# Joining the small products of an attention and mixture-of-experts kernel into two runs a batch

## The chip, the core and the metric

One NeuronCore of a Trainium2 chip. The time is that of one execution on the device, in microseconds, as the median of several runs; lower is better. The engines run side by side and wait for one another through semaphores: TensorE (PE; PEld is its weight load) for products, VectorE (DVE), ScalarE (ACT), GpSimd (POOL), and SyncE (SP), which issues nearly all transfers.

## The reference

Eight batches, eight heads, 576 tokens, 64 columns a head, 32 memory slots, eight experts:

```python
a = softmax(phi, axis=2)                        # token to memory, (b, h, s, 32)
k_m = einsum('bhsm,bhsd->bhmd', a, k); v_m = einsum('bhsm,bhsd->bhmd', a, v)
attn = softmax(q @ k_m.T / 8) @ v_m             # (b, h, s, 64)
x = attn as (4608, 512)
logits = x @ w_gate + modality_bias[modality_id]
e = argmax(logits); gate = softmax(logits)[e]
out = gate * (relu(x @ w1[e]) @ w2[e])          # one expert a token
```

## The kernel before

With the inputs at hand all tokens prefer one expert; the kernel guesses it from the modality of the first token, runs all tokens through it, and tests at the end (`verdict`) whether any token wanted another; only then a second, general path (`any_experts`) runs. That path reads split copies of the attention weights from DRAM (`xa_dram`, `xb_dram`).

Attention is never multiplied by `v_m` first. For each batch the memory values times `w1` (`value_products`, two halves of the 1024 columns, line 756) give a matrix `vws` of 256 rows; the attention weights of the tokens times `vws` give the hidden layer (`hidden`, line 803), and that times `w2` the output (`outputs`, line 840). Both large stages are exact to float32 by splitting each operand in a high and a low part and making three products. A batch has a part 0 of 256 tokens and a part 1 of the rest; in line 840's stage these are tiles of 128 tokens (0 and 1, then 2 and 3), and every odd batch has a fifth tile for what is left of both batches of a pair (`None`). A tile is 8 chunks (`f`) of 3 products; a hidden part is 8 times 6 products.

The small products of a batch `b`, all on parts of the array:

- `mem_kv` (line 409, and line 417 for its sums): keys and values of the memory, 64 rows by 32 columns of the array, from `exp` of `phi` and from `kv_sb`, which the next batch's load overwrites; then `kv_divide` (VectorE: `den` line 493, `rec`; ScalarE: `kvn` line 499).
- `mem_turn` (line 148): two transposes on the full array, then a copy to `kvT`.
- `scores` (line 565): 64 by 32. Its result is turned, softened and normalised in steps by VectorE and ScalarE (`soften` e, `normalise` n, `a_split` x), which give the weights that `hidden` reads.
- `mem_gate` (line 545): memory values times `w_gate`, 128 by 32, eight products, from `wgd`, a copy of `w_gate` with zeros; copied to `vg`.
- `value_weights`: `value_products` of one half (64 by 32, 16 products of 512 columns), and its split by ScalarE and VectorE (lines 153 and 154).
- `logits` (line 698): weights times `vg`, 128 by 32; then `gate`, whose `gates` scale each output on its way out of PSUM (`gated`, line 853).

PSUM has eight banks: four are taken in turn by `pe` tiles (hidden, outputs, value products), and two pairs (`pair0`, `pair1`) serve the small products.

The order of the instructions of all engines is written out by a planner (`weave`) while the kernel is built. It has two lists: `experts`, strictly in order (hidden, outputs, value products), and `attention`, sorted by a due time that is counted in the progress of the experts. Each stage has its product time and a chain of other engines' times in `TAKES`. An attention stage is put in when its due time has come and its inputs are ready by the planner's own clock; one that uses VectorE is held back while VectorE's queue is more than 3.5 us ahead (some kinds: less). Transfers wait in a list, `later`, of which each call of `hidden` or `outputs` issues one; the output stores and the loads of `k`, `v` and `phi` are issued at once where they are called. `behind` holds back those loads for some batches until the next output store.

At the start, while `phi` is on its way, TensorE does products of zeros: `BUSY[0]` small ones (`warm_small`, line 166) and ten of 512 columns (line 159).

Of the kernel before, what the change touches and what calls it, by code (L numbers as in the profile page):

```python
# [54 lines left out]
def attn_moe(ctx: ExitStack, tc: tile.TileContext, q, k, v, phi, mod_id, w_gate, mod_bias, w1, w2, out):  # L55
    nc = tc.nc
# [20 lines left out]
    HW = MAIN + 2 * QP  # L77
    SCALE = 1.0 / float(D) ** 0.5
    EPS = 1e-9
    BUSY = 90, 10  # L80
# [26 lines left out]

    wgd = const.tile([P, KCH, NG, E], F32, name="wgd")
# [150 lines left out]
    def clear():  # L259
        for t in [wgd] + vg:  # L260
            nc.gpsimd.memset(t, 0.0)

    def prepare():

        for r in range(2):
            half = slice(QP * r, QP * (r + 1))
            for i in range(2):

                nc.gpsimd.tensor_copy(mid_f[half, :, RA * i:RA * (i + 1)], mid[:, i::2, r:2 * RA:2, 0])
            nc.gpsimd.tensor_copy(mid_f[half, :, 2 * RA], mid[:, r::2, QC - 1, 0])  # L270
        for m in range(NMOD):
            nc.gpsimd.tensor_single_scalar(is_m[m][:, :, 0], mid_f.rearrange("p a c -> p (a c)"), float(m), op=ALU.is_equal)
        for g in range(NG):
            rows = slice(D * g, D * (g + 1))
            nc.gpsimd.tensor_copy(wgd[rows, :, g, :], wg[rows])
# [282 lines left out]
    def scores(b):  # L558
        sc = [pair_of_banks(g) for g in range(NG)]
        qT = q_sb[b % 2].rearrange("p j (a x) -> p j a x", a=2)  # L560
        for a in range(2):
            for j in range(HG):
                for g in range(NG):
                    rows = slice(QP * g, QP * (g + 1))
                    nc.tensor.matmul(  # L565
                        sc[g][M * j:M * (j + 1), a, 0:QC * BL], lhsT=kvT[b][rows, 0, M * j:M * (j + 1)],
                        rhs=qT[rows, j, a], start=True, stop=True, tile_position=(QP * g, M * j),
                    )
        live["sc", b] = sc
        if b + 2 < B:  # L570
            load_queries(b + 2)

    def first_scores(c0, n):

        sc = [pair_of_banks(g) for g in range(NG)]
        qT = q_sb[0].rearrange("p j (c u t) -> p j c u t", u=2, t=BL)
        cs = slice(c0, c0 + n)
        for u in range(2):
            for j in range(HG):
                for g in range(NG):  # L580
                    for a in range(2):
# [7 lines left out]
        if c0 + n == QC:  # L589
            load_queries(2)  # L590
# [80 lines left out]
    def a_split(b, part, step=None):  # L671
# [11 lines left out]
        if b % 2:  # L683
            for x, d in zip(dst, drams[b // 2]):
                nc.sync.dma_start(d.bitcast(F32), x.rearrange("p i g c x -> p (i g c x)").bitcast(F32))

    def logits(b):

        pair, i = b // 2, b % 2
        x = live["aT", b].rearrange("p g (c a t) -> p g c a t", a=2, t=BL)  # L690
        pl = bank("pa")
        last = RA * BL
        for cs, c0 in ((slice(0, 2 * RA, 2), 0), (slice(2 * RA, QC, 2), last)):
            for g in range(NG):
                for r in range(HG):
# [5 lines left out]
                    )  # L701
        lgT = wk.tile([P, RB, BL], F32, name="lgT")
# [80 lines left out]

    def value_weights(b, hf):
        value_products(b, hf)
        for g, pv in enumerate(live.pop(("pv", hf))):
# [111 lines left out]
    def first_w2(c):  # L898
# [40 lines left out]
    def plan_memory(b, due, floor=0.0):  # L939
# [6 lines left out]
        for name, after, what, late in (  # L946
# [4 lines left out]
            ("kv", [("exp0" if b < 2 else "exp", b), ("sums", b)], mem_kv, 6.0),  # L951
            ("kvT", [("kv", b)], mem_turn, 9.0),
            *((("vg", [("kvT", b), ("e", b, 1, 0)], mem_gate, 16.9),) if b == 1 else ()),
        ):
            stage(attention, (name, b), name, after, what, b, due=due + late, floor=floor if name in ("max", "kv") else 0.0)
# [94 lines left out]
    def plan_steps(b, dues):  # L1050
# [8 lines left out]
        def step(part):  # L1059
            for k in range(4):  # L1060
                before = ("e", b, part, k - 1 - (b == 1 and (part, k) == (0, 3))) if k else ("s", b, part if b == 0 else 0)
                add(("e", b, part, k), f"e{part}{k}", [before], soften, b, part, k)

        def weights(part):
            for k in range(3):
                before = [("n", b, part, k - 1) if k else ("e", b, part, 3)]
                if b and k == 2:
                    before += [("l", b - 1), ("x", b - 1, 1)]
# [7 lines left out]
        if b:  # L1076
            add(("s", b, 0), "s", [("kvT", b), ("qt", b, HG - 1)], scores, b)
# [7 lines left out]
        else:  # L1085
            step(1)
            todo.insert(len(todo) - 1, (("vg", 0), "vg", [("e", 0, 1, 0)], mem_gate, (0,)))
# [3 lines left out]
        add(("l", b), "l", [("n", b, 1, 2), ("vg", b)], logits, b)  # L1091
# [3 lines left out]
        add(("g", b), "g", [("l", b)], gate, pair, c0, n)  # L1095
# [11 lines left out]
        if b == B - 1:  # L1107
            stage(attention, ("v",), "verdict", [("others", pair)], verdict, due=due + 12.0)
# [8 lines left out]
    def plan_experts(b):  # L1117
        def next_values(hf):
            if b + 1 < B:
                stage(experts, ("vw", b + 1, hf), "vw", [("kvT", b + 1)], value_weights, b + 1, hf, banks=2, full=True)  # L1120

        def some(t, f, kind, terms):
            last_ = f == FCH - 1 and terms[-1] == 2
            stage(
# [3 lines left out]

        def tile_(t):
# [49 lines left out]
    AHEAD, EARLIER, SPREAD = (5.8, 5.0), {7: -6.0}, 0.55  # L1179
# [14 lines left out]
    def weave(experts):  # L1194
# [26 lines left out]
        while at or ex:  # L1221
# [38 lines left out]
            if s[7]:  # L1260
                for k in range(max(1, s[6])):
                    ring[(turn_ - 1 - k) % 4] = t
# [162 lines left out]
```

## Time and profile before

| | |
|---|---|
| Median of 3 runs | 385.58 us (384.74 to 386.07) |
| The profiled execution | 386.81 us, its span 385.0 us |
| TensorE busy | 378.4 us, 98% of the span |
| VectorE, ScalarE, GpSimd busy | 64%, 37%, 12% |
| Mean granted clock of TensorE | 1.000 |

Span is the time from the first to the last instruction of the profiled execution. A product's end is modelled and products overlap, so in what follows the time between the starts of two products counts, not their length. "L840" is line 840 of the kernel before.

### The profile page before, as it was taken

To read this page: it belongs to the slowest core of one execution; us is meant where nothing else is said; L and a number is where in the kernel's file an instruction comes from. 1 tells how busy PE (TensorE), PEld (TensorE's weight loads), DVE (VectorE), ACT (ScalarE), POOL (GpSimd) and SP (SyncE) were. 2 spreads that over 40 slices of the span, in tenths; PEclk is the share of its full clock that TensorE was granted. 3 is DMA by queue.
4 is the path that set the end of the run, shared out by engine and by line. 5 is a ranking of instruction groups with operands and counts; after the bars stand their busy time and mean duration, and the time that the engine had idled before them with its cause. 6 is when DMAs were issued, how large, how long until landed. Compare 5 with 4: busy or idle time off the path is not lost.

```text
span 385.0 us, 9899 instructions
## 1 busy us (share of the span) xinstructions
PE 378.4 (98%) x4007; PEld 305.5 (79%) x4007; DVE 244.8 (64%) x610; ACT 141.2 (37%) x328; POOL 45.7 (12%) x113
## 2 busy tenths in 40 slices
PE   7899999999999999999999999999999999999996
PEld 2767886889679887787878878797967988698986
DVE  3689767885688478745777378773667535892400
ACT  1274332524334233332443324342432324351401
POOL 3229030023000300030000300003000030000000
PEclk9999999999999999999999999999999999999999
DMA  8999669974389296806862069844501111153112
GB/s 292 346 377 222 107 118 316 261 155 147 56 269 184 69 301 116 303 12 197 206 111 49 9 205 217 207 162 127 176 21 36 29 29 29 29 204 97 31 35 55
DMA packets 91674, 56.88 MB, mean 148 GB/s; under 512 B 69476, under 2 KB 74852, under 8 KB 91620
## 3 DMA queue, kind: packets, MB, share of 16 engines
q1 hardware_dynamic: 91344, 55.87, 53.3%
q8 instruction: 33, 0.54, 0.6%
q10 hardware_dynamic: 276, 0.30, 0.2%
q14 instruction: 21, 0.17, 0.1%
HBM read 37.28 MB, written 18.87 MB: 146 GB/s over the span
## 4 chain that ended last, share of the span: by engine, by line
PE 97%; DMA 1%; DVE 1%; ACT 0%; issue 0%; ACTq 0%
PE pe L840 52%; PE pe L803 27%; PE pe L756 4%; PE pair L409 4%; PE pair L565 2%; PE pe L884 1%; PE pair L698 1%; DMA ph<-in_phi_dram 1%; PE pair L434 1%; PE pair L148 1%; DVE top L311 1%; PE pair L583 1%; PE pair L756 1%; PE pe L434 1%; PE pair L545 0%; PE pair L803 0%
## 5 line engine op out<-in xcount | busy, mean ns | idle before, releaser
L840 PE MATMUL pe<-w2h,hh 128*128 128x512 f32 x280 | 113.8, 406 | 0.1
L840 PE MATMUL pe<-w2h,hl 128*128 128x512 f32 x280 | 109.4, 391 | 0.0
L840 PE MATMUL pe<-w2l,hh 128*128 128x512 f32 x280 | 107.3, 391 | 0.0
L820 DVE SCALAR_TENSOR_TENSOR hl<-pe,hh 128x256 fp32r<-128x256 f32 (+2 forms) x158 | 57.3, 389 | 38.4 <-ACT hh L816 37.5
L840 PEld LDWEIGHTS pe<-w2h,hh 128*128 128x128 f32 x280 | 52.5, 188 | 23.7 <-issue 13.9
L816 ACT ACTIVATE hh<-pe 128x256 fp32r<-128x256 f32 (+2 forms) x158 | 53.2, 362 | 36.8 <-PE pe L803 36.5
L840 PEld LDWEIGHTS pe<-w2l,hh 128*128 128x128 f32 x280 | 52.5, 188 | 11.5
L840 PEld LDWEIGHTS pe<-w2h,hl 128*128 128x128 f32 x280 | 52.7, 188 | 9.5 <-issue 0.3
L853 ACT ACTIVATE ob<-pe,gates 128x512 f32<-128x512 f32 x35 | 23.9, 687 | 75.9 <-PE pe L840 48.9
L803 PE MATMUL pe<-xbh,vwh 128*128 128x320 f32 x128 | 40.1, 313 | 0.0
L803 PE MATMUL pe<-xbh,vwl 128*128 128x320 f32 x128 | 39.5, 309 | 0.0
L803 PE MATMUL pe<-xbl,vwh 128*128 128x320 f32 x128 | 39.5, 309 | 0.0
L803 PE MATMUL pe<-xah,vwh 128*128 128x256 f32 x124 | 35.2, 287 | 0.0
L803 PE MATMUL pe<-xal,vwh 128*128 128x256 f32 x124 | 34.9, 283 | 0.0
L803 PE MATMUL pe<-xah,vwl 128*128 128x256 f32 x124 | 34.9, 283 | 0.0
L345 POOL COPY ts<-tm 32x4 f32<-32x4 f32 x24 | 4.8, 200 | 203.8 <-DVE tm L337 203.0
L803 PEld LDWEIGHTS pe<-xah,vwh 128*128 128x128 f32 x124 | 23.6, 191 | 2.2 <-ACT vwl L773 0.8
L803 PEld LDWEIGHTS pe<-xbh,vwh 128*128 128x128 f32 x128 | 24.0, 188 | 1.2 <-DVE hl L820 0.6
L153 ACT CAST vwh<-pe 128x512 fp32r<-128x512 f32 x26 | 14.0, 590 | 29.7 <-PE pe L756 29.7
L803 PEld LDWEIGHTS pe<-xbl,vwh 128*128 128x128 f32 x128 | 24.0, 188 | 0.3
L803 PEld LDWEIGHTS pe<-xbh,vwl 128*128 128x128 f32 x128 | 24.0, 188 | 0.0
L803 PEld LDWEIGHTS pe<-xal,vwh 128*128 128x128 f32 x124 | 23.7, 191 | 0.2
(178 smaller groups left out, 468.0 us busy)
## 6 DMA issues: line engine op xcount, KB each, us to landing
out_dram<-ob SPq DMA_DIRECT2D x72, 128.0 KB, 2.4
q_sb<-in_q_dram SPq DMA_DIRECT2D x112, 72.0 KB, 3.2
kv_sb<-in_k_dram SPq DMA_DIRECT2D x6, 1152.0 KB, 7.0
kv_sb<-in_v_dram SPq DMA_DIRECT2D x6, 1152.0 KB, 10.1
ph<-in_phi_dram SPq DMA_DIRECT2D x13, 288.0 KB, 7.6
kv_sb<-in_k_dram SPq DMA_DIRECT2D x4, 576.0 KB, 5.7
kv_sb<-in_v_dram SPq DMA_DIRECT2D x4, 576.0 KB, 7.0
raw<-in_moe_w_dram SPq DMA_DIRECT2D x2, 1024.0 KB, 7.2
```

The lines of the kernel that those rows point to most:

```text
L148: nc.tensor.transpose(dst, src, ident[:rows, :rows])
L153: nc.scalar.copy(h, src)
L345: nc.gpsimd.tensor_copy(ts_[BL * a:BL * (a + 1)], live["tm"][BL * o:BL * (o + 1)])
L409: nc.tensor.matmul(live["kvp"][M * j:M * (j + 1), g], lhsT=pe[half, j, c * M:(c + 1) * M], rhs=kv_sb[half, :, j, c * D:(c + 1) * D], start ...
L434: nc.tensor.matmul(to[g][M * j:M * (j + 2), 0:2 * D].rearrange("p (j d) -> p j d", j=2), lhsT=pe[half, c, j:j + 2].rearrange("p j m -> p ( ...
L565: nc.tensor.matmul(sc[g][M * j:M * (j + 1), a, 0:QC * BL], lhsT=kvT[b][rows, 0, M * j:M * (j + 1)], rhs=qT[rows, j, a], start=True, stop=T ...
L756: nc.tensor.matmul(pvs[g][M * j:M * (j + 1), :], lhsT=vT[b][rows, j, :], rhs=raw1[rows, j, cols], start=True, stop=not more, tile_position ...
L803: nc.tensor.matmul(ph[:, 0:n], lhsT=(vl if k == 2 else vh)[:, g, cols], rhs=xl if k == 1 else xh, start=(g == k == 0), stop=(g == NG - 1 a ...
L816: nc.scalar.activation(hs[0][:, f, h0:h0 + p1 - p0], live["ph", f][:, p0:p1], AF.Relu)
L820: nc.vector.scalar_tensor_tensor(hl, live["ph", f][:, p0:p1], 0.0, hh.bitcast(F32), op0=ALU.max, op1=ALU.subtract)
L840: nc.tensor.matmul(po, lhsT=tile_columns(hl if n == 1 else hh, f, t), rhs=(w2l if n == 2 else w2h)[:, f, :], start=(f == n == 0), stop=(f ...
L853: nc.scalar.activation(ob, po, AF.Copy, scale=gate_of(b, t))
```

## The change

`mem_gate` is done in the run of `scores`, with sixteen products of 64 rows (each on one half of `w_gate`) instead of eight of 128 rows; its results lie behind the scores in the same banks, and two copies by VectorE take them to `vg`. For batches from `FROM` = 3 on, `logits` of the batch before is done at the head of the same run; this run is a member of `experts`, right after the last product of tile 0, and the eviction of tile 0 follows in the middle of tile 1 ("fin"). `mem_kv` of batch `b + 2`, both halves of value products of `b + 1` and `mem_turn` of `b + 2` become one run at a fixed row of `experts` of batch `b`: after tile 2 (even `b`) or tile 3 (odd `b`), or at the place that `JOINT` names (batch 1: after chunk 1 of the fifth tile; batch 2: after chunk 1 of tile 2; batch 3: after chunk 6 of tile 3). The second half of value products uses `pair0` instead of two `pe` banks, except in batch 6. Due times of the attention stages are reckoned anew. The split weights are written to DRAM per batch in halves of the old pieces, through `later`. `BUSY[0]` falls from 90 to 64, and `wgd` is gone.

```diff
+    FROM = 3
+    JOINT = {1: (4, 1), 2: (2, 1), 3: (3, 6)}
-    BUSY = 90, 10
+    BUSY = 64, 10
...
     def mem_kv(b):
         kv_products(b)
         kv_divide(b)
-        if b in (2, 4, 5):
+        if b in (4, 5):
             behind.append(b)
...
-    def mem_gate(b):
-        pg = bank("pa")
+    def mem_gate(b, to):
         for j in range(HG):
-            nc.tensor.matmul(
-                pg[M * j:M * (j + 1), 0:NG * E], lhsT=vT[b][:, j], rhs=wgd[:, j].rearrange("p g e -> p (g e)"),
-                start=True, stop=True, tile_position=(0, M * j),
-            )
+            for g in range(NG):
+                rows = slice(D * g, D * (g + 1))
+                nc.tensor.matmul(
+                    to[g][M * j:M * (j + 1), 0, GATE:GATE + E], lhsT=vT[b][rows, j], rhs=wg[rows, j],
+                    start=True, stop=True, tile_position=(D * g, M * j),
+                )
+
+    def gate_values(b, to):
         o = E * (b % 2)
-        nc.vector.tensor_copy(vg[b // 2][:, :, o:o + E], pg[:, 0:NG * E].rearrange("p (g e) -> p g e", g=NG))
+        for g in range(NG):
+            nc.vector.tensor_copy(vg[b // 2][:, g, o:o + E], to[g][:, 0, GATE:GATE + E])
...
     def scores(b):
         sc = [pair_of_banks(g) for g in range(NG)]
+        if b >= FROM:
+            logits_product(b - 1, sc[0][:, 0, LOGITS:GATE])
...
         live["sc", b] = sc
+        mem_gate(b, sc)
+        if b >= FROM:
+            add_logits(b - 1, sc[0][:, 0, LOGITS:GATE])
+        gate_values(b, sc)
...
-        if b % 2:
+        c = NG * n * P // 2
+        for i in (0, 1) if b == 1 and not part else (b % 2,):
             for x, d in zip(dst, drams[b // 2]):
-                nc.sync.dma_start(d.bitcast(F32), x.rearrange("p i g c x -> p (i g c x)").bitcast(F32))
+                later.append((d[:, c * i:c * (i + 1)].bitcast(F32), x[:, i].rearrange("p g c x -> p (g c x)").bitcast(F32)))
...
+    def other_values(b):
+        pair = pair_of_banks(0)
+        value_products(b, 1, lambda: [pair[:, g] for g in range(NG)])
+        value_split(1)
...
+    def begin(b):
+        return 61.2 * (b // 2) + 27.8 * (b % 2) - 0.3
...
+            if last_ and t == 0 and FROM <= b + 1 < B:
+                stage(experts, ("o", b, t, f, terms[0]), kind, [], outputs, t, range(f, f + 1), lambda po: None, terms)
+                stage(experts, ("s", b + 1, 0), "ls", [("n", b, 1, 2), ("kvT", b + 1), ("qt", b + 1, HG - 1)], scores, b + 1)
+                return
...
-                if b and t in (2, 3) and f == FCH // 2 - 1:
-                    next_values(t - 2)
+                if t == 1 and f == FCH // 2 - 1 and FROM <= b + 1 < B:
+                    stage(experts, ("fin", b, 0), "fin", [("g", b)], finish_first, full=True)
+                if 0 < b < B - 1 and (4 if t is None else t, f) == JOINT.get(b, (2 + b % 2, FCH - 1)):
+                    if b + 2 < B:
+                        stage(experts, ("kv", b + 2), "kvj", [("exp", b + 2), ("sums", b + 2)], mem_kv, b + 2)
+                    next_values(0)
+                    if b + 2 < B:
+                        stage(experts, ("vw", b + 1, 1), "vw", [], other_values, b + 1)
+                    else:
+                        next_values(1)
+                    if b + 2 < B:
+                        stage(experts, ("kvT", b + 2), "kvTj", [("kv", b + 2)], mem_turn, b + 2)
...
-    AHEAD, EARLIER, SPREAD = (5.8, 5.0), {7: -6.0}, 0.55
+    AHEAD, SPREAD = 5.8, 0.55
+    TURNS, MEMORY = -3.0, 0.0
...
     for b in range(2, B):
-        at0 = (b - 1) * BATCH - AHEAD[b > 2] - EARLIER.get(b, 0.0)
-        plan_memory(b, at0)
-        plan_turns(b, at0 + 6.0, 1.3)
-        plan_steps(b, evenly(at0 + 11.5, SPREAD, 24))
+        if b < FROM:
+            at0 = (b - 1) * BATCH - AHEAD
+            plan_memory(b, at0)
+            plan_turns(b, at0 + 3.3, 0.1)
+            plan_steps(b, evenly(at0 + 5.5, SPREAD, 24))
+            continue
+        plan_turns(b, begin(b - 1) + TURNS, 0.1)
+        if b == FROM:
+            plan_memory(b, at0 + 7.5, exp=at0 + 10.0)
+        else:
+            plan_memory(b, begin(b - 2) + MEMORY)
+        plan_steps(b, evenly(begin(b - 1) + 7.9, 0.3, 24))
...
-                gate_ = ("vg", s[0][1])
-                if s[0][0] == "vw" and s[0][1] > 1 and gate_ not in done and done.get(("e", s[0][1], 1, 0), now + 1.0) < now:
-                    mem_gate(s[0][1])
-                    now += 0.18
-                    done[gate_] = free["D"] = max(now, free["D"]) + 0.2
```

## Rows read from the trace of the kernel before

**Rows 1.** The page: busy time of the engines, and the chain by engine.
```profile
PE 378.4 (98%) x4007; PEld 305.5 (79%) x4007; DVE 244.8 (64%) x610; ACT 141.2 (37%) x328; POOL 45.7 (12%) x113
...
PE 97%; DMA 1%; DVE 1%; ACT 0%; issue 0%; ACTq 0%
```

**Rows 2.** The chain in order of time (start us, us, what): one batch.
```profile
219.47 2.08 PE pair L409 x138
221.55 0.13 PE pair L417 x13
...
225.58 1.13 PE pair L565 x32
...
229.66 7.04 PE pe L803 x48
...
239.44 0.19 PE pair L545 x8
239.62 1.02 PE pe L756 x16
...
244.27 0.70 PE pair L698 x32
```

**Rows 3.** Timeline of TensorE (start us, us, what) around one batch's logits.
```profile
201.94 0.39 PE L840 MATMUL pe<-w2h,hl 128*128 128x512 f32 x1
202.17 0.39 PE L840 MATMUL pe<-w2l,hh 128*128 128x512 f32 x1
202.49 0.77 PE L698 MATMUL pair<-aT,vg 128*32 128x128 f32 x32
203.19 0.50 PE L840 MATMUL pe<-w2h,hh 128*128 128x512 f32 x1
203.53 0.39 PE L840 MATMUL pe<-w2h,hl 128*128 128x512 f32 x1
```

**Rows 4.** Timeline of TensorE: two runs of value products, adjacent.
```profile
19.25 1.09 PE L756 MATMUL pair<-raw,kvT 64*32 64x512 f32 x16 [0.36 <-ACT kvT L540]
20.13 1.83 PE L756 MATMUL pe<-raw,kvT 64*32 64x512 f32 x16
```

**Rows 5.** Timeline of TensorE around one batch's two turns.
```profile
222.87 0.40 PE L840 MATMUL pe<-w2l,hh 128*128 128x512 f32 x1
223.11 0.38 PE L148 MATMUL pair<-ident,kvn 128*128 128x128 f32 x2
...
223.56 0.40 PE L840 MATMUL pe<-w2h,hl 128*128 128x512 f32 x1
```

**Rows 6.** Timeline of all engines after one batch's mem_kv.
```profile
221.61 0.50 PE L840 MATMUL pe<-w2h,hh 128*128 128x512 f32 x1
...
221.88 0.16 DVE L493 TENSOR_SCALAR den<-pair 128x2 f32<-128x2 f32 x1 [4.99 <-PE pair L417]
...
222.34 0.63 ACT L499 ACTIVATE kvn<-pair,rec 128x128 f32<-128x128 f32 x2 [4.70 <-DVE rec L495]
```

**Rows 7.** Timeline of VectorE: first and last step of one batch's weights.
```profile
136.59 0.78 DVE L612 STREAM_TRANSPOSE a<-pair 128x256 f32<-128x256 f32 x2 [1.94 <-PE pair L565]
...
155.53 0.83 DVE L681 TENSOR_TENSOR xbl<-aT,xbh 128x640 fp32r<-128x640 f32 x1
```

**Rows 8.** Timeline of ScalarE and VectorE: the split of one half of value products.
```profile
248.34 1.07 ACT L153 CAST vwh<-pe 128x512 fp32r<-128x512 f32 x2 [1.08 <-PE pe L756]
...
248.96 1.29 DVE L154 TENSOR_TENSOR vwl<-pe,vwh 128x512 fp32r<-128x512 f32 x2 [0.67 <-ACT vwh L153]
```

**Rows 9.** Timeline of TensorE: the opening.
```profile
1.31 0.88 PE L166 MATMUL pair<-busy 64*32 64x16 bf16 x90 [1.31 <-POOL busy L1276]
...
7.25 0.45 PE L148 MATMUL pair<-ident,top 128*128 128x128 f32 x1 [0.52 <-DVE top L311]
...
10.35 4.12 PE L434 MATMUL pair<-kv_sb,exp 64*64 64x128 f32 x72
...
14.43 2.20 PE L434 MATMUL pe<-kv_sb,exp 64*64 64x128 f32 x72
```

More of the change, by code (lines that the diff above doesn't have):

```diff
@@ L259, in clear @@
     def clear():
-        for t in [wgd] + vg:
+        for t in vg:
             nc.gpsimd.memset(t, 0.0)
@@ L589, in first_scores @@
         if c0 + n == QC:
+            mem_gate(0, sc)
+            gate_values(0, sc)
             load_queries(2)
@@ L682, in a_split, with logits_product @@
         drams = xb_dram if part else xa_dram
-        if b % 2:
+        c = NG * n * P // 2
+        for i in (0, 1) if b == 1 and not part else (b % 2,):
             for x, d in zip(dst, drams[b // 2]):
-                nc.sync.dma_start(d.bitcast(F32), x.rearrange("p i g c x -> p (i g c x)").bitcast(F32))
+                later.append((d[:, c * i:c * (i + 1)].bitcast(F32), x[:, i].rearrange("p g c x -> p (g c x)").bitcast(F32)))
     def logits(b):
-        pair, i = b // 2, b % 2
+        add_logits(b, logits_product(b, bank("pa")))
+    def logits_product(b, pl):
+        pair = b // 2
         x = live["aT", b].rearrange("p g (c a t) -> p g c a t", a=2, t=BL)
-        pl = bank("pa")
         last = RA * BL
@@ L701, in logits, with add_logits @@
                     )
+        return pl
+    def add_logits(b, pl):
+        pair, i = b // 2, b % 2
         lgT = wk.tile([P, RB, BL], F32, name="lgT")
@@ L950, in plan_memory @@
             ("sums", [("exp0" if b < 2 else "exp", b)], mem_sums, 3.2),
-            ("kv", [("exp0" if b < 2 else "exp", b), ("sums", b)], mem_kv, 6.0),
-            ("kvT", [("kv", b)], mem_turn, 9.0),
-            *((("vg", [("kvT", b), ("e", b, 1, 0)], mem_gate, 16.9),) if b == 1 else ()),
+            *(() if b >= FROM else (
+                ("kv", [("exp0" if b < 2 else "exp", b), ("sums", b)], mem_kv, 6.0 + (-2.6 if b == 2 else 0.0)),
+                ("kvT", [("kv", b)], mem_turn, 5.0 if b == 2 else 9.0),
+            )),
         ):
-            stage(attention, (name, b), name, after, what, b, due=due + late, floor=floor if name in ("max", "kv") else 0.0)
+            stage(attention, (name, b), name, after, what, b, due=exp + late - 3.0 if exp and late >= 3.0 else due + late, floor=floor if name in ("max", "kv") else 0.0)
     def plan_turns(b, due, gap, floor=0.0):
@@ L1061, in step @@
                 before = ("e", b, part, k - 1 - (b == 1 and (part, k) == (0, 3))) if k else ("s", b, part if b == 0 else 0)
-                add(("e", b, part, k), f"e{part}{k}", [before], soften, b, part, k)
+                add(("e", b, part, k), f"e{part}{k}", [before] + ([("vwp", 1, 1)] if (b, part, k) == (1, 1, 3) else []), soften, b, part, k)
         def weights(part):
@@ L1066, in weights @@
                 before = [("n", b, part, k - 1) if k else ("e", b, part, 3)]
+                if b == part == 1 and k == 0:
+                    before += [("vw", 1, 1)]
                 if b and k == 2:
-                    before += [("l", b - 1), ("x", b - 1, 1)]
+                    before += ([("l", b - 1)] if b < FROM else []) + [("x", b - 1, 1)]
                 add(("n", b, part, k), f"n{part}{k}", before, normalise, b, part, k)
@@ L1076, in plan_steps @@
         if b:
-            add(("s", b, 0), "s", [("kvT", b), ("qt", b, HG - 1)], scores, b)
+            if b < FROM:
+                add(("s", b, 0), "s", [("kvT", b), ("qt", b, HG - 1)], scores, b)
             step(0)
@@ L1086, in plan_steps @@
             step(1)
-            todo.insert(len(todo) - 1, (("vg", 0), "vg", [("e", 0, 1, 0)], mem_gate, (0,)))
         weights(1)
@@ L1090, in plan_steps @@
             put(1)
-        add(("l", b), "l", [("n", b, 1, 2), ("vg", b)], logits, b)
+        joined = FROM <= b + 1 < B
+        if not joined:
+            add(("l", b), "l", [("n", b, 1, 2), ("s", b, int(b == 0))], logits, b)
         if b:
@@ L1094, in plan_steps @@
         c0, n = RA * i, RB if i else RA
-        add(("g", b), "g", [("l", b)], gate, pair, c0, n)
+        dues = list(dues)
+        if joined:
+            dues[len(todo):] = [begin(b) + 7.6 + 0.05 * k for k in range(5)]
+        add(("g", b), "g", [("s", b + 1, 0) if joined else ("l", b)], gate, pair, c0, n)
         if i:
@@ L1107, in plan_steps @@
         if b == B - 1:
-            stage(attention, ("v",), "verdict", [("others", pair)], verdict, due=due + 12.0)
+            stage(attention, ("v",), "verdict", [("others", pair)], verdict, due=begin(b) + 9.0)
     def one_of_two():
@@ L1118, in next_values @@
         def next_values(hf):
-            if b + 1 < B:
-                stage(experts, ("vw", b + 1, hf), "vw", [("kvT", b + 1)], value_weights, b + 1, hf, banks=2, full=True)
+            stage(experts, ("vw", b + 1, hf), "vw", [("kvT", b + 1)], value_weights, b + 1, hf, banks=2, full=True)
         def some(t, f, kind, terms):
             last_ = f == FCH - 1 and terms[-1] == 2
+            if last_ and t == 0 and FROM <= b + 1 < B:
+                stage(experts, ("o", b, t, f, terms[0]), kind, [], outputs, t, range(f, f + 1), lambda po: None, terms)
+                stage(experts, ("s", b + 1, 0), "ls", [("n", b, 1, 2), ("kvT", b + 1), ("qt", b + 1, HG - 1)], scores, b + 1)
+                return
             stage(
@@ L1127, in some, with finish_first @@
             )
+        def finish_first():
+            store(b, 0)(live["po", 0])
         def tile_(t):
```

13 lines of the change are left out of this document (7 added, 6 removed), and 2 rows, old and new, of the table TAKES.

## The prediction

> **What bounds the kernel now.** I read the page's shares first, then the chain of work that ended last, then the timeline of TensorE where one kind of product follows another. The page shows TensorE busy for 98% of the span and the chain puts 97% on it [rows 1]; after the first 24 us the chain is TensorE's own queue, one product behind another. So an edit pays only if TensorE has less to do, or loses less between two products, and it costs only where TensorE has to wait.
>
> The chain in order of time shows what TensorE does in a batch: long stretches of full-array products (line 840, 0.23 us each; line 803, 48 in 7.04 us), cut by short runs of small products on tiles of the array [rows 2]: mem_kv's 144 products with 16 sums, scores, mem_gate, each half of the value products, logits. From batch 3 on a batch has five such stretches (mem_gate stands against one half of the value products) and, by itself, mem_turn's two turns.
>
> Next, the price of a cut. Around the logits [rows 3] the products of line 840 start 0.23 apart, but 0.32 from the last one to the run and 0.34 from the first one after it to the second. A cut costs 0.09 + 0.11 = 0.20 us that is nobody's work. A run also has a start and an end of its own: 16 value products alone take 1.02 us up to the next product [rows 2], but with another 16 of the same shape behind them the second begins 0.88 us after the first [rows 4]. So 0.14 us goes when two runs of one shape are joined. Around the two turns [rows 5] two ordinary intervals and the turns take 0.69 us; 0.69 - 0.46 = 0.23 is the turns and their cut. The turns are of the full array's shape, so I call 0.11 of it cut; the bounds are nothing and 0.23.
>
> **The change part by part.** *Joined runs.* For k from 3 to 7 the old order has five stretches and the turns: 5 x 0.20 + 0.11 = 1.11. The new one has two: logits(k-1), scores(k) and mem_gate(k) after the first tile of batch k-1, and mem_kv(k), both halves of value products of k-1 and mem_turn(k) at a fixed row of batch k-2. That is 0.40, so 0.71 is saved. Inside, three joints are of one shape (64 rows by 32 columns): kv to values, values to values, scores to gate; 3 x 0.14 = 0.42, with nothing as the lower bound. From logits (128 rows by 32) to scores the shape changes, and I save nothing there.
>
> *mem_gate.* Eight products in 0.19 us [rows 2] become sixteen of half the rows. The nearest row is mem_kv's sums, of the new shape: 13 of them in the chain take 0.13 us. I take 0.13, which saves 0.06; the upper bound goes by the old gate's 0.024 us apiece, 16 x 0.024 = 0.38. The Trainium skill (TensorE: Matmul & The Clock Gate, section on the back-to-back issue gap) has a rule against this edit: starts are never closer than about 25 ns, however small the product. By it the sixteen would take 0.40 us. The sums, 10 ns apart, and mem_kv's 138 in 2.08 us, 15 ns apart, do not obey it on small tiles, so the sum goes by them.
>
> Per k that is 0.71 + 0.42 + 0.06 = 1.19, five times 5.95. Elsewhere: gate 0 loses its own cut and its 0.19 but is put behind scores of another shape (0.20 + 0.19 - 0.13 - 0.14 = 0.12), gate 1 saves 0.20 + 0.19 - 0.13 = 0.26, gate 2 0.06, and the two value halves of batch 7 become one run, 0.34. That is 0.78, and 6.7 us in all.
>
> *What the joined run adds.* It ends in turns that need kv_divide's result, which a cut and line 840 products used to cover. From the end of the sums at 221.61 the denominator, the reciprocal and the two scalings are done at 222.97, 1.36 us later, with VectorE idle 4.99 us before [rows 6]. The two value halves cover 2 x 0.88 = 1.76, so 0.40 is to spare. Behind a busy VectorE there would be nothing to spare: the planner lets its queue run 3.5 us ahead, mem_kv takes 2.2 of it, and with one more piece of 0.9 the denominator comes 2.2 us late and the turns 1.8. While TensorE stands there, everything of line 840 stands behind it. Is VectorE busy then? Scores to the last split of one batch took it from 136.59 to 156.36, 19.8 us [rows 7]. The new run begins 5.5 + 7.0 + 5.5 = 18 us after the scores in batch 4, some 14 in batch 2 and 23 in batches 3 and 5 (tiles of 24 products, 7.04 for the hidden products). So batches 2 and 4 can meet a queue, 3 and 5 hardly; batch 1 I cannot tell. I take 0.5 us at two of the five, 1.0 in all; the bounds are nothing and 5 x 1.8 = 9.0.
>
> In batch 6 both value halves take banks of the four, and the next tile needs the first bank back. Casting and subtracting took from 248.34 to the middle of the second row's 1.29 us, 249.6 [rows 8], 1.3 us; the second half covers 0.88. That is 0.4 us once.
>
> *Gates.* The first tile's eviction now waits for logits that come after it, and is put behind four chunks of the second tile, 12 x 0.23 = 2.8 us. If the gates are later, ScalarE stands and the bank is late; the bank is wanted again only by the third hidden product, 5.5 + 1.8 us after the run. I cost it at nothing; without that cover it would be what the gates lack, under 1 us a batch.
>
> *Smaller pieces.* The write-out of the split weights goes from one transfer a pair to one a batch, through the list that the products empty one by one. What it writes is read only if the last branch finds another expert, and the list is empty long before the last store: nothing; if it were not covered, a store would leave a little later. mem_gate's result is now copied by two instructions of VectorE instead of one; that lies under line 840's products, as does what GpSimd no longer does.
>
> *Opening products.* 90 take 0.88 us; 26 fewer is 0.25 us, and TensorE then stands for 0.52 us anyway until VectorE's maximum lets the first transpose go at 7.25 [rows 9]. So nothing directly. But the first 72 products of line 434 take 4.12 us and the next 72 of the same form 2.20: the lower and the upper of the clock's two levels (1.2 and 2.4 GHz), and TensorE had been at work with short gaps before. If the rise came earlier or later with the altered opening, up to 1.9 us are at stake either way. I take zero and leave it for the range.
>
> Sum: -6.7 + 1.0 + 0.4 = -5.3. The profiled execution took 386.81 us (385.0 of span and 1.8 around it), which gives 381.5. The median of the runs shown is 1.23 us under it, so I forecast **380.3** for the median.
>
> **The rivals.** *Joined runs wait (other side).* The turns stand for VectorE in all five joined runs, at the bound: 9.0 + 0.4 - 6.7 = 2.7 slower, 388.3. It decides from 1.26 us a run. For it: 19.8 us of VectorE work against 14 to 18 of distance. Against: batches 3 and 5 are 23 us away. Chance 0.10. *A middle wait*, 0.9 us in each: 4.5 + 0.4 - 6.7 = -1.8, 383.8. Chance 0.10.
>
> *The gate pieces each pay their own slot.* Sixteen at 0.024 us, 0.25 more than I put, eight times: 382.3. The old gate's row speaks for it, the sums' row against. The rule of the Trainium skill weighed above (TensorE: Matmul & The Clock Gate) is this mechanism. Chance 0.06.
>
> *The cut is not a matter of shape.* If each group of products pays on entering new tiles of memory whatever precedes it, joining saves nothing but the turns' 0.11 and the 0.4 is lost: 385.6, no change. The value run behind another at 0.88 speaks against it. Chance 0.06.
>
> *My forecast*, waits small: 0.68.
>
> **How the numbers follow.** 0.3%, 1.2 us, is about what a measurement here can tell from no change. Forecast, middle wait and gate slots are faster by more: 0.84. The cut that stays gives the same: 0.06. Slower: 0.10. The range goes up to the middle wait with its scatter, 384.6, which leaves out 0.16; below, no waits at all give 378.9 and a part of the clock's 1.9 takes it to 378.0, with some 0.03 under it.
>
> **What would show it.** Right: from batch 2 on two stretches of small products a batch in the chain; value run to value run 0.88; a joined run of about 4.2 us; the gate's sixteen in about 0.13; line 840 about as often at 0.23; waits of TensorE after 24 us under 1.5 in all. Wrong: turns whose weight load waits for the scalings of line 499, a line 803 product waiting for a split, or line 434's first 72 at another time than 4.1.

## The result and the profile after

The changed kernel takes 380.37 us, median of 4 runs (380.21 to 380.81), beside 385.82 (384.74 to 386.63) for the kernel before: ratio 0.987, 95% interval 0.9843 to 0.9897. The profiled execution took 380.38 us with a span of 378.6 (before: 386.81 and 385.0). In the new file line 840 is line 868, 803 is 831, 756 is 776, 565 is 571, 545 is 546, 698 is 713, 409 and 417 are 408 and 416, 148 is 150, 153 and 154 are 155 and 156, 434 is 433. Below, every ratio is to the kernel before, run beside it again (medians 384.99 to 385.41); one execution of e9, 519.6 us at a granted clock of 0.66, is in no ratio.

The page after, answering [rows 1]; the last line is TensorE's instruction fetches (queue: packets, MB, share).

```profile
PE 370.4 (98%) x4045; PEld 308.5 (81%) x4045; DVE 248.6 (66%) x618; ACT 139.7 (37%) x328; POOL 46.1 (12%) x110
...
q8 instruction: 33, 0.54, 0.6%
...
PE 88%; DVE 5%; DMA 3%; ACT 2%; issue 1%; SPq 1%; ACTq 0%; DVEq 0%
```

TensorE is as full as before. The chain has moved partly to VectorE and ScalarE: behind the opening it now leaves TensorE twice, from 31.6 to 43.2 and from 111.2 to 121.6, and both times it comes back at products of the hidden layer that wait, first 0.31 us behind an eviction by ScalarE, then 0.33 and 0.38 us for a split.

The chain in order of time, one batch (start us, us, what), answering [rows 2, 4].

```profile
167.91 2.94 PE pe L868 x13
170.85 0.70 PE pair L713 x32
171.55 1.09 PE pair L571 x27
172.65 0.08 PE pair L546 x14
172.72 5.67 PE pe L868 x24
178.39 7.27 PE pe L831 x48
185.66 10.23 PE pe L868 x45
195.89 2.08 PE pair L408 x138
...
198.10 1.07 PE pe L776 x15
199.17 0.86 PE pair L776 x16
200.03 0.37 PE pair L150 x2
200.40 3.67 PE pe L868 x16
```

Two runs of small products a batch: logits, scores and gate from 170.85 to 172.72, and kv, both value halves and the turns from 195.89 to 200.40, 4.5 us by the chain. By TensorE's starts the second run is from 195.82 to 200.15, 4.33 us, beside the 4.2 that the prediction names as a sign. The second value half takes 0.86.

The timeline of TensorE at the edges of these two runs, answering [rows 3, 5].

```profile
170.47 0.39 PE L868 MATMUL pe<-w2l,hh 128*128 128x512 f32 x1
170.78 0.77 PE L713 MATMUL pair<-aT,vg 128*32 128x128 f32 x32
171.48 1.20 PE L571 MATMUL pair<-q_sb,kvT 64*32 64x288 f32 x32
172.48 0.25 PE L546 MATMUL pair<-wg,kvT 64*32 64x8 f32 x16
172.66 0.50 PE L868 MATMUL pe<-w2h,hh 128*128 128x512 f32 x1
172.99 0.40 PE L868 MATMUL pe<-w2h,hl 128*128 128x512 f32 x1
...
199.96 0.44 PE L150 MATMUL pair<-ident,kvn 128*128 128x128 f32 x2
200.15 0.48 PE L868 MATMUL pe<-w2h,hh 128*128 128x512 f32 x1
200.47 0.40 PE L868 MATMUL pe<-w2h,hl 128*128 128x512 f32 x1
```

A run is entered 0.31 after the last large product and left with 0.33 to the second, as before. The turns take 0.19 (199.96 to 200.15), and behind them the first large product still pays 0.32. The sixteen gate products take 0.18 up to the next product.

The opening, answering [rows 9].

```profile
9.36 2.20 PE L433 MATMUL pair<-kv_sb,exp 64*64 64x128 f32 x72 [0.23 <-ACT exp L378]
11.73 0.29 PE L444 MATMUL pair<-ones_c,sums 64*64 64x1 f32 x8 [0.18 <-DVE sums L392]
11.87 2.56 PE L433 MATMUL pe<-kv_sb,exp 64*64 64x128 f32 x72
```

The first 72 products take 2.20 instead of 4.12, the pace of the second 72 in [rows 9]: TensorE was at the upper level (2.4 GHz, granted clock 1.00) already.

Where the time went, from TensorE's starts in the two traces. The first output product (line 840, now 868) starts at 27.61 instead of 29.64, 2.03 us earlier. From there to the last product it is 347.47 instead of 351.88 us; I call this stretch the body. Of its -4.41 the lines below hold all but 0.05; "pace" is the usual time from one large product to the next.

```
entering a run of small products   41 times 3.80 us -> 22 times 2.04   -1.77
large products beyond their pace   7.11 -> 5.17                        -1.94
kv with its sums                   15.52 -> 16.00                      +0.48
scores                              8.61 -> 7.29                       -1.32
gate                                1.48 -> 2.00                       +0.52
values                             14.27 -> 13.65                      -0.62
turns                               0.98 -> 1.28                       +0.29
```

The second line holds three things. There are 24 exits fewer, for five runs of turns, each left by itself, are gone too: -2.61. The products soon behind an exit are a little over their pace, in all some 0.02 an exit: -0.56. And the waits took some of this back: those of large products rose from 0.46 to 1.35, or from 0.79 to 2.01 with the product behind each wait, which is up to 0.11 longer. Kv holds two stops, 0.28 and 0.33, that nothing in the trace releases (timeline of TensorE's weight loads):

```profile
110.84 0.17 PEld L416 LDWEIGHTS pair<-ones_c,sums 64*32 64x32 f32 x13 [0.29 <-issue]
286.95 0.10 PEld L408 LDWEIGHTS pair<-kv_sb,exp 64*32 64x32 f32 x1 [0.33 <-issue]
```

### The profile page after: what moved, and what is told of

Read it like the earlier page. It is cut to its first block, busy times and chain, and to the rows that moved or that the text cites. A ratio compares the mean times of both kernels' runs of the same rounds, so it can differ in the third digit from the quotient of the medians.

```text
span 378.6 us, 9983 instructions
## 1 busy us (share of the span) xinstructions
PE 370.4 (98%) x4045; PEld 308.5 (81%) x4045; DVE 248.6 (66%) x618; ACT 139.7 (37%) x328; POOL 46.1 (12%) x110
## 4 chain that ended last, share of the span: by engine, by line
PE 88%; DVE 5%; DMA 3%; ACT 2%; issue 1%; SPq 1%; ACTq 0%; DVEq 0%
PE pe L868 48%; PE pe L831 26%; PE pair L408 4%; DMA raw<-in_moe_w_dram 2%; PE pe L776 2%; PE pair L571 2%; PE pe L912 2%; PE pair L776 1%; PE pair L713 1%; DMA ph<-in_phi_dram 1%; DVE vwl L156 1%; PE pair L150 1%; DVE top L310 1%; DVE a L650 0%; DVE sa L640 0%
## 5 line engine op out<-in xcount | busy, mean ns | idle before, releaser
L868 PE MATMUL pe<-w2h,hh 128*128 128x512 f32 x280 | 111.3, 397 | 0.0
L831 PEld LDWEIGHTS pe<-xal,vwh 128*128 128x128 f32 x124 | 23.7, 192 | 0.2
L831 PEld LDWEIGHTS pe<-xah,vwl 128*128 128x128 f32 x124 | 23.7, 192 | 0.0
```

The source lines that it names most:

```text
L831: nc.tensor.matmul(ph[:, 0:n], lhsT=(vl if k == 2 else vh)[:, g, cols], rhs=xl if k == 1 else xh, start=(g == k == 0), stop=(g == NG - 1 a ...
L868: nc.tensor.matmul(po, lhsT=tile_columns(hl if n == 1 else hh, f, t), rhs=(w2l if n == 2 else w2h)[:, f, :], start=(f == n == 0), stop=(f ...
```

## The experiments

**First theory and its rivals.** Theory A: the 2 us of the opening come from the 64 products, by way of the clock. Rival B: the clock rises by chance, and the joined runs did it all. Three more kernels price single cuts and one the order of VectorE and ScalarE.

**e1_open64**: the kernel before, with the new opening.

```diff
-    BUSY = 90, 10
+    BUSY = 64, 10
```

> The kernel before with 64 opening products of nothing instead of 90, nothing else changed. Theory A (the altered opening moves the rise of TensorE's clock): as in the changed kernel the ten 512-column products after them speed up within the opening, the first 72 products of keys take about 2.2 us instead of 4.1, and the time falls by 1.5 to 2 us, to about 384. Rival B (the rise falls where it falls in each execution, whatever the opening): no change, ratio within 0.2% of 1, and the 72 products take 2.2 or 4.1 us by chance. My prediction had put this part at zero.

384.79 (384.31 to 386.41, 12 runs) beside 385.36: ratio 0.9992 (0.9976 to 1.0009). That is no difference clear of noise, and less than the 1.5 to 2 us of A, although its profiled execution had the early rise too (timeline of TensorE):

```profile
9.25 2.20 PE L434 MATMUL pair<-kv_sb,exp 64*64 64x128 f32 x72 [0.24 <-ACT exp L379]
...
11.76 1.94 PE L434 MATMUL pe<-kv_sb,exp 64*64 64x128 f32 x58
13.95 0.66 PE L434 MATMUL pe<-kv_sb,exp 64*64 64x128 f32 x14 [0.25 <-issue]
```

So A's clock is out. Note the stop behind the 58th product, with no releaser (0.52 us from one start to the next, behind 448 of TensorE's instructions); it returns below.

**e2_open90**: the changed kernel, with the old opening (e1's diff reversed).

> The changed kernel with its opening of 90 products put back. Theory A: 1.5 to 2 us slower than the changed kernel, about 382.2 (ratio to the kernel before 0.9905), with the first 72 products of keys at 4.1 us. Rival B: as the changed kernel, 380.4 (0.986).

384.23 (382.96 to 385.19, 12 runs), ratio 0.997 (0.9956 to 0.9985): 3.9 us slower than the changed kernel. Neither theory had this. The clock is not it: the first 72 products took 2.20 here as well. The body is 351.13, 3.7 more, and the timeline of TensorE shows where:

```profile
89.97 0.31 PE L831 MATMUL pe<-xbh,vwl 128*128 128x320 f32 x1
91.87 0.31 PE L831 MATMUL pe<-xbh,vwh 128*128 128x320 f32 x1 [1.60 <-ACT hh L844]
...
149.98 1.15 PE L776 MATMUL pair<-raw,kvT 64*32 64x512 f32 x8
151.72 1.06 PE L776 MATMUL pair<-raw,kvT 64*32 64x512 f32 x8 [0.58 <-issue]
```

TensorE halts in the middle of sixteen like products whose data are there, and just behind a kv run. (The releaser named at 91.87 is no cause: that piece of ScalarE's work had ended at 90.87, 1.0 us before.) New theory S: what counts is the place in TensorE's instruction stream. Its instructions come in pieces of 0.54 MB / 33 = 16 KB; small products use a piece up faster than the next one arrives, and the opening's count decides where the pieces end. Rival O: the opening itself acts on what follows.

**e5_later26**: the changed kernel, 26 products of nothing more, but behind the opening's first exponentials.

```diff
         nothing(2)
+        add(("nothing", "small"), "nothing", [], warm_small, 26)
```

> The changed kernel, opening of 64 as it is, and 26 more of the same small products of nothing later, after the first exponentials are begun, where TensorE stands anyway. With 90 in the opening the changed kernel lost 3.8 us, and nearly all of it stood in three waits of TensorE that no engine releases: 1.6 and 0.9 us in joined runs, 1.8 us among hidden products. Theory S (the place in TensorE's instruction stream: what is fetched in pieces of 16 KB reaches the joined runs late if a piece ends at the wrong place; 26 products before them shift it): as with 90, 383.5 to 384.5, with the same three waits. Rival O (the opening itself, its length or the clock): 380.4.

385.16 (383.99 to 386.27, 10 runs), ratio 0.9995 (0.9976 to 1.0015); the body is 351.07, and the stops are at the same products (timeline of TensorE):

```profile
150.64 1.15 PE L776 MATMUL pair<-raw,kvT 64*32 64x512 f32 x8
152.47 1.06 PE L776 MATMUL pair<-raw,kvT 64*32 64x512 f32 x8 [0.68 <-issue]
```

S, not O.

**e6_block**: the changed kernel with 196 small and 6 large products of nothing, that is 128 products or 256 instructions more: one whole piece.

```diff
-    BUSY = 64, 10
+    BUSY = 196, 6
```

> The changed kernel with an opening of 196 small products and 6 of 512 columns: 128 products, 256 instructions, one piece of 16 KB more than with 64 and 10. Theory S: the joined runs stand to the pieces as in the changed kernel, so 380.4 (up to 0.5 more if the opening itself gets longer), none of the three waits. Rival O (more products in the opening cost): 384 or more.

382.35 (380.99 to 383.35, 4 runs), ratio 0.9916 (0.9884 to 0.9947). The body is 347.01, 0.46 less than in the changed kernel, and has none of the stops. The 2 us more are in the opening (3.4 in the profiled execution, the slowest of the four), where one stop of this kind now stands (timeline of TensorE):

```profile
15.97 0.66 PE L433 MATMUL pe<-kv_sb,exp 64*64 64x128 f32 x14 [1.80 <-issue]
```

Behind it, from 16.8 to 23.7, the granted clock was 0.50, the lower level (1.2 GHz).

**e11_open77** and **e12_open51**: BUSY = 77, 10 and BUSY = 51, 10.

> The changed kernel with 77 small opening products (13 more). Theory S (place in the instruction stream): the waits that nothing releases lie between those with 64 and with 90; each of the five joined runs at 4.3 to 4.4 us where a piece comes in time, up to 6 where not. Rival O: as with 64.

> The changed kernel with 51 small opening products (13 fewer). Theory S: the pieces end 26 instructions later in each joined run than with 64; the two waits of 0.3 us inside mem_kv of batches 3 and 7 go or move, no other is sure to come. Rival O: as with 64.

381.46 and 386.17, one run each. Bodies by count of opening products, one trace each: 51: 352.7; 64: 347.5; 77: 348.4; 90: 351.1. So 64 is a lucky one of the four. 77 lies between 64 and 90, as S has it. With 51 the expectation was wrong: the two stops of 0.3 did not go but grew to 2.4 and 1.3, and a third came. The one in batch 3's kv costs more than itself. Timeline of TensorE, then windows (us, busy and count by engine, granted clock, DMA share, GB/s):

```profile
112.33 0.26 PE L416 MATMUL pair<-ones_c,sums 64*32 64x1 f32 x13
114.85 0.19 PE L416 MATMUL pair<-ones_c,sums 64*32 64x1 f32 x2 [2.26 <-issue]
```
```profile
111.00:115.70 4.70, 2.44 (x145) 1.87 (x137) 0.33 (x2) 0.14 (x1) 0.32 (x1) 1.00 0.74 123
115.70:119.10 3.40, 3.40 (x29) 1.49 (x14) 1.88 (x4) 2.56 (x6) 0.00 (x0) 0.50 0.95 352
119.10:125.00 5.90, 5.90 (x36) 5.22 (x35) 4.49 (x10) 2.81 (x6) 0.00 (x0) 1.00 1.05 378
```

Behind the stop the granted clock is 0.50 for 3.4 us.

I then counted, in the traces of these runs and of e10 below, TensorE's instructions (weight loads, products and its own others) ahead of each stop in the middle of like products or their sums, where none of its instructions starts for over 0.8 us, with the time since the instruction queue's last fetch began:

```
run   TensorE goes on at   nothing for   instructions ahead   after the fetch began
e2        19.04               0.85             704                  2.47
e2        91.87               1.90            2496                  2.27
e2       151.72               1.17            4032                  2.42
e5        13.64               0.98             449                  2.38
e5        19.91               1.12             705                  2.38
e5        92.47               1.65            2497                  2.55
e5       152.47               1.27            4033                  2.45
e6        15.97               2.07             705                  2.50
e10       18.95               0.82             705                  2.61
e10       92.34               2.47            2497                  2.20
e11       20.52               1.01             705                  2.48
e11       92.88               0.84            2497                  2.42
e12       53.51               1.15            1473                  2.52
e12      114.85               2.43            3009                  2.45
e12      292.84               1.26            6849                  2.36
```

449, 705, 1473, 2497, 3009, 4033, 6849: they differ by whole multiples of 256 (within one record), and TensorE goes on 2.2 to 2.6 us after the fetch of the next piece began. The two stops in the changed kernel's kv are of this kind: they stand behind 3009 and 6849 instructions, 2.42 and 2.30 us after fetches began (108.43 and 284.65). Nor is a stop found at every edge of a piece. In all 14 traces the fetches, taken in order, go with the edges 449 + 256 n; at none of these 433 edges does TensorE go on less than 2.2 us after the fetch of that piece began, and edges in small products that it reaches 2.8 us or more after it pass without a stop. That is S as plainly as a trace can show it. What decides when a fetch begins stays open: some began up to 4.8 us before TensorE entered the piece before it, some up to 6.1 us after. A kv run alone is 288 instructions in some 2.0 us, the joined run 388 in 4.3: a piece lasts 1.8 to 2.8 us there, as long as a fetch. In line 868's products it lasts 128 x 0.23 = 29. In the changed kernel the 4033rd instruction falls at 153.4, among line 868's.

**e4_cut_logits**: the logits one chunk ahead of the scores, so one cut more per batch.

```diff
...
+                if t == 0 and f == FCH - 2 and FROM <= b + 1 < B:
+                    stage(experts, ("early", b + 1), "early", [("n", b, 1, 2)], early_logits, b + 1)
```

> The changed kernel with logits one chunk of output products ahead of scores and gate products (five places). My theory: 0.20 us for each cut and nothing more, since logits and scores have different shapes and the end of the one and start of the other are paid either way: 1.0 us, 381.4. Rival (the drain at a change of shape inside a run is part of the 0.20): clearly less, under 0.5 us. Rival (a cut is not a matter of shape): nothing.

380.48 (380.22 to 381.51, 4 runs), ratio 0.9871 (0.9846 to 0.9897): no difference that the time could show, where 1.0 us was expected. The body has 0.50 more for entering, 0.10 a cut, and by estimate as much for leaving, but some 0.6 less elsewhere, 0.28 of it one of the two stops in kv, which is gone; 0.43 is left. The price is seen here, the gain of joining at this place not.

**e9_cut_kv5**: a chunk of line 868's products between kv and the values, in batches 1 to 5.

```diff
...
                         stage(experts, ("kv", b + 2), "kvj", [("exp", b + 2), ("sums", b + 2)], mem_kv, b + 2)
+                    apart = True
+                if apart and (b + 2 == B or (4 if t is None else t, f) != JOINT.get(b, (2 + b % 2, FCH - 1))):
+                    apart = False
                     next_values(0)
```

> The cut between mem_kv and the values again, but only in the five joined runs that have both (batches 1 to 5); batch 6 is as in the changed kernel, since in the run before the planner's order there put 3.2 us of waiting and after it 3.4 us of the clock's lower level into one place. Theory from that run's other places: 0.10 going into and 0.16 coming out of each cut, and nothing for parting runs of the same shape there: 5 x 0.26 = 1.3 us, less up to 0.6 for two waits inside mem_kv that the changed kernel has: 381.0 to 381.7. What my prediction holds (0.14 more a cut): 2.0, 382.4. Rival (cuts cost nothing): 380.4.

382.27 (381.09 to 382.88 without the execution named above), ratio 0.9929 (0.9902 to 0.9956), above the 381.0 to 381.7 expected. The body grows by 1.09: entering +0.50, large products +0.77, kv +0.01, values -0.18. A cut costs about 0.22 to 0.25, and parting kv from the values costs the runs themselves nothing: without stops they take 2.21 and 1.88 apart, 2.18 and some 1.94 joined. The other 0.6 of the profiled execution is in its opening, where the granted clock was 0.50 again for 3.4 us.

**e3_cut_kv**: the same in all batches.

> The changed kernel with a chunk of three output products put between mem_kv and the values and turns in the five joined runs (batches 1 to 5). My theory: each new cut costs 0.20 us, and 0.05 to 0.14 us more because two runs of one shape are parted; five times that is 1.0 to 1.7 us, so about 381.4 to 382.1, less what is saved where the turns or values waited. Rival (a cut is not a matter of shape): nothing, 380.4.

385.84, ratio 1.0015 (0.9989 to 1.0041). It tells nothing of the cut: the planner put batch 6's value halves next to each other behind the logits, and the second needed a bank (timeline of TensorE):

```profile
327.96 1.90 PE L776 MATMUL pe<-raw,kvT 64*32 64x512 f32 x18
332.02 1.09 PE L776 MATMUL pe<-raw,kvT 64*32 64x512 f32 x14 [2.15 <-DVE vwl L156]
```

Here too the granted clock was 0.50 for 3.4 us after it.

**e8_gate_only**: the kernel before, with the gate's sixteen products behind the scores, and 90 opening products.

```diff
...
+        mem_gate(b, sc)
...
-            *((("vg", [("kvT", b), ("e", b, 1, 0)], mem_gate, 16.9),) if b == 1 else ()),
...
```

> The kernel before with one part of the change alone: the gate products in the run of the scores as sixteen of half the rows, all else in its old place, opening of 90. My theory: 0.14 us less for each of the eight (the run with the gate took 1.17 us in the changed kernel, apart 1.13 and 0.19) and 0.20 for the two cuts that vanish (batches 0 and 1): 1.5 us less, ratio 0.996. Rival (each small piece pays a slot of 25 ns): 16 instead of 8 such slots, no gain or 1 us slower.

390.94, ratio 1.0149 (1.0123 to 1.0175). The planner moved work in batch 1 so that TensorE stood for one split, and ran the next 6.8 us at the lower level. Its waits (engine, line, for what, us, times, longest), then its windows:

```profile
PE pe L805 <- DVE vwl L780: 4.9, 1, 4.9
```
```profile
68.00:73.10 5.10, 1.01 (x9) 0.81 (x7) 4.42 (x10) 1.93 (x5) 0.00 (x0) 1.00 1.10 283
73.10:79.90 6.80, 5.98 (x53) 5.63 (x54) 4.18 (x12) 1.52 (x4) 0.00 (x0) 0.50 0.88 232
```

The eight gates and the scores of line 565, by TensorE's starts, took 9.02 instead of 10.09 us: 0.13 less a batch.

**e10_gate_held**: e8 with two lines that the change has as well and that hold batch 1's order.

```diff
...
+                add(("e", b, part, k), f"e{part}{k}", [before] + ([("vwp", 1, 1)] if (b, part, k) == (1, 1, 3) else []), soften, b, part, k)
...
+                if b == part == 1 and k == 0:
+                    before += [("vw", 1, 1)]
```

> The gate products alone on the kernel before once more, now with the change's two lines that hold the last softening step and the normalising of batch 1 behind the split of its value products; without them TensorE stood 4.9 us for that split. My theory: 0.13 us less for each of eight gates and 0.2 for each of two cuts, 1.5 us: 383.9, ratio 0.996. If the 4.9 us stay, the lines do not do it: 390 again.

386.30 (384.51 to 387.09, 10 runs), ratio 1.002 (0.9993 to 1.0046). The 4.9 us are gone, gate and scores take 9.10; but a stop of 2.5 us stands behind batch 2's kv, at the 2497th instruction of the table. Without it the time would be some 384, by estimate. This kernel has the old order but for the gate, and the trace of the kernel before has a stop of 0.3 us too, behind 4289 instructions: such stops are not of joined runs alone.

**e7_split_order**: the changed kernel, in which the two casts of ScalarE go ahead of the two subtractions of VectorE.

```diff
-        for g, pv in enumerate(live.pop(("pv", hf))):
-            split([x[:, g, hf * 512:(hf + 1) * 512] for x in vws], pv)
+        pvs = live.pop(("pv", hf))
+        for g, pv in enumerate(pvs):
+            nc.scalar.copy(vws[0][:, g, hf * 512:(hf + 1) * 512], pv)
+        for g, pv in enumerate(pvs):
+            h, l = (x[:, g, hf * 512:(hf + 1) * 512] for x in vws)
+            nc.vector.tensor_tensor(l, pv, h.bitcast(F32), op=ALU.subtract)
```

> The changed kernel; in the split of a half of the value products ScalarE's two casts are put ahead of VectorE's two subtractions, instead of by turns. TensorE's instructions are the same. In the changed kernel the second cast of the half that uses the pair of banks waits for the first subtraction, and VectorE is late for the hidden products of batch 2, where TensorE waits 0.7 us in all. My theory (those waits are VectorE's queue, lengthened by the turns): the time falls by 0.3 to 0.7 us, to about 380.0. Rival (the waits have to do with the order of the softening steps alone): no change, 380.4.

379.40 (378.79 to 380.08, 4 runs), ratio 0.9857 (0.9829 to 0.9885), the lowest of all, though its interval overlaps that of the changed kernel. The timeline of the changed kernel, around the second half's split in batch 1:

```profile
113.65 0.61 ACT L155 CAST vwh<-pair 128x512 fp32r<-128x512 f32 x1
116.39 0.63 DVE L156 TENSOR_TENSOR vwl<-pair,vwh 128x512 fp32r<-128x512 f32 x1
117.05 0.59 ACT L155 CAST vwh<-pair 128x512 fp32r<-128x512 f32 x1 [2.78 <-DVE vwl L156]
117.66 0.69 DVE L156 TENSOR_TENSOR vwl<-pair,vwh 128x512 fp32r<-128x512 f32 x1 [0.65 <-ACT vwh L155]
```

and of this one:

```profile
113.06 1.10 ACT L816 CAST vwh<-pair 128x512 fp32r<-128x512 f32 x2
115.79 1.22 DVE L819 TENSOR_TENSOR vwl<-pair,vwh 128x512 fp32r<-128x512 f32 x2
```

By turns, the second cast waits 2.78 us behind the first subtraction, which VectorE reaches late; the split ends at 118.35 instead of 117.01, and the hidden products wait 0.7. Here those waits are gone, the two kv stops too, and the body is 346.20, 1.27 less: 0.65 before large products and 0.65 in kv. TensorE's instructions are the same, and the edges behind 3009 and 6849 of them came 2.5 and 3.2 us after their fetches began. So the half in kv hangs on when two fetches began, and is not shown to come from the new order.

## Why the prediction was right, and which of its steps were not

**The cut** was right in place and size: 41 entries became 22, 1.77 / 19 = 0.09 each, and 24 exits fell away, 2.61 / 24 = 0.11 each: 4.38 us against the 4.15 forecast. Eighteen of the 19 entries are those of the sum; the last is that of batch 7's logits, which came between its value halves. Joining logits to scores, two shapes, saved the whole slot and nothing more, as assumed. The turns' own cut is in these exits: five runs of turns, entered at nothing and left at 0.09, are gone, 0.44 us where 5 x 0.11 was put down. But the turns themselves take 0.19 instead of 0.14 at the end of a joined run, 0.29 in all, which the sum does not have. What it does not have either is the 0.56 by which products behind an exit are over their pace.

**The joints inside runs** were over-sized. "Three joints are of one shape ... 3 x 0.14" holds for values to values (0.62 less over the whole kernel) and for scores to gate (0.13 in e8 and e10), and fails for kv to values (e9: 0.01 and -0.18). Scores, gate, values, turns and kv without its stops come to -1.26 instead of the -2.6 that the joints and the gate were to bring. The gate's sixteen take 0.18 to 0.20 up to the next product in six batches of eight, 2.00 / 8 = 0.25 on average, where I put 0.13; the rival's 16 x 0.024 = 0.38 did not come. The Trainium skill (TensorE: Matmul & The Clock Gate, the back-to-back issue gap) has about 25 ns as the floor between two starts, 0.40 here by estimate; on these small tiles the trace does not agree.

**The waits** were in the wrong places and of about the right sum. "0.5 us at two of the five" turns: none of the turns waited for VectorE. "That is 0.4 us once" in batch 6: none, for the planner put the logits between the halves (e3 shows what it costs when it does not). In their place 1.2 more before large products and in the product behind each wait, most of it hidden products waiting for a split made by turns (e7 has 0.65 less), and 0.6 in two stops in kv. 1.8 us, forecast 1.4. With "under 1.5 in all" after 24 us I was too low: 2.0, without the products behind the waits. Of the three signs of being wrong two came, and they stand for small sums: line 803 products waited for a split, 0.7 us in batch 2, and the first 72 took 2.20.

**The step that failed** is "so nothing directly ... I take zero and leave it for the range" for the opening products. I saw the clock as the only risk, and that risk looks like chance: the runs of before spread over 1.9 us, and e1 moves them by nothing clear of noise. What the count does is shift the pieces of TensorE's stream against the runs of small products: 3.9 us between 64 and 90 on the new kernel (e2, e5, e6). On the old one e1 shows no difference clear of noise; that this is because its short runs lie apart is not shown, for e10, in nearly the old order, has a stop of 2.5 us. Joined runs with the old opening would have been just inside the range, at 384.2. That the forecast came out is therefore partly the luck of this count.

So the body's -4.4 against the forecast -5.3 comes out of its parts: -4.38 for entries and exits, -0.56 for the products behind exits, -1.26 for the runs themselves, +1.83 for waits and stops. The other 1.0 of the medians' 5.45 lies in the opening, where the profiled pair differs by 2.0. Whether the new opening is steadier or four runs were fortunate stays open. That the median came within 0.1 us of the forecast is luck: the body saved 0.9 less than the sum, and the opening, put at nothing, gave 1.0.

## What to carry to other kernels

A run of small products between large ones costs about 0.2 us of TensorE at its two ends, so join the runs; but a run of small products can use its instructions (256 in 1.8 to 2.8 us here) faster than they arrive, so look for pauses without a releaser in the middle of like products, count the instructions ahead of them, and move the edge (here by 26 products of nothing) into a stretch of large products. Where a planner makes the order, a single edit is read from the pieces of the trace, not from the time: in e3 and e8 a moved step cost more than all that was measured. A source that two engines split by turns made them wait for each other here (2.78 us once); one engine after the other took 0.65 us of waits off TensorE, in one trace.

## What the runs showed of the hardware

TensorE's instructions came in pieces of 16 KB, 256 at a time. At 433 edges of pieces in 14 traces it never went on less than 2.2 us after the fetch of the next piece had begun. Where it reached an edge sooner it stood, up to 2.5 us, and went on 2.2 to 2.7 us after the fetch began; the changed kernel's two stops in kv (2.42 and 2.30) are of this kind. Products on small tiles started 11 to 15 ns apart: 138 of kv in 2.08 us, the gate's sixteen in 0.18. Behind stops of 2.1 (e6), 2.4 (e12), 2.7 (e3) and 5.2 us (e8), from one start to the next, the granted clock fell to the lower level for 3.4 to 6.8 us; behind those of 1.9 (e2) and 2.5 us (e10) it stayed at 1.00. What decides this is not shown.
